# Another order of steps and of PSUM banks in the first part of an attention and Fourier-mix kernel

## Chip, cores and metric

The kernel runs on one core of a Trainium2 chip. The metric is the device time of one execution in microseconds (us), the median over several runs. Engines: TensorE (PE), VectorE (DVE), ScalarE (ACT), GpSimd (POOL) and SyncE (SP), which issues the DMAs.

## What is computed

Eight batches, eight heads, 576 positions, 64 dimensions per head; 128 random features; all float32 (the two MLP weights come as float64). First a linear attention with positive features, then a Fourier mix with residual, a layer norm and an MLP with residual:

```python
def phi(x):
    proj = np.einsum('bhsd,md->bhsm', x, omega)
    sq = np.sum(x * x, axis=-1, keepdims=True) / 2.0
    h = proj - sq
    h = h - np.max(h, axis=-1, keepdims=True)
    return np.exp(h) / np.sqrt(m)
q_p, k_p = (phi(q_s), phi(k_s))
kv = np.einsum('bhsm,bhsd->bhmd', k_p, v)
z = np.sum(k_p, axis=2)
num = np.einsum('bhsm,bhmd->bhsd', q_p, kv)
den = np.einsum('bhsm,bhm->bhs', q_p, z)[..., None] + 1e-06
x = (num / den) transposed and reshaped to (B, S, H*D)

u = x + np.real(np.fft.fft(np.fft.fft(x, axis=1), axis=2))
un = (u - mean(u)) / np.sqrt(var(u) + 1e-06)
out = u + np.maximum(un @ w_ch1, 0.0) @ w_ch2
```

## The kernel before

The kernel has two parts. Part one (to about 418 us of the profile) does the attention and the Fourier mix of all eight batches, converts the MLP's weights to float32, and does the MLP of the first four tiles of 128 rows. Part two does the MLP of the other 4096 rows in blocks, with sums of sub-blocks that save products (Strassen's way).

Part one works on 32 pairs of heads, n = 0 to 31, four to a batch. Its work is written as streams of steps: Python generators that yield a `Step` (engine, estimated duration, what it waits for, which buffers it takes and gives back) and then issue the step's instructions. The steps that matter here, with the names that the text uses and the lines at which the profile lists them:

- `T kqTn a:b`: PE transposes columns a to b of k and q of pair n into one PSUM bank (L636). ACT or DVE copies the bank to SBUF (L652, L650).
- `Sn a:b`: scores against the features (L731), four matmuls on quarters of the array for each column, or two on halves of its rows (the form R). `Sn 0:4` and `Sn 5:9` fill two banks, `Sn 4:5` is narrow but takes two banks as well. DVE takes the maximum over the features (nmx, L673: wide over two banks, or narrow), ACT the exponentials (L690), four to a bank. The banks come free behind them.
- `KVn`: 36 small matmuls (72 records) of the keys' features with v and a column of ones (L766) into two banks. ACT or DVE copies the result (L782, L780).
- `T qeTn a:b`: transposes the queries' features (L636), copied by L652 or L650.
- `NDn`: numerator and denominator (L814, L822) into two banks. DVE adds the epsilon, takes the reciprocal (rden, L831, L832) and multiplies (L843, or ACT at L839); that frees the two banks.
- `MIXb`: the Fourier mix of batch b as matmuls with tables (L933, L947, then L993, L1004), after sums on DVE and POOL (L870 to L910); DVE adds the results (L1047 to L1060).
- `Pj hf` and `Pj of`: hidden and output steps of the plain MLP of tile j (L1293, L1318), closed by an addition on DVE (L1332).
- `narrow`: the conversion of one 128x512 piece of a weight from float64, 32 pieces, on POOL or ACT (L558, L560), then DVE (L563, L565, L568, L570), then POOL or DVE (L576).
- `warm`: 12 records of matmuls on zeros at the beginning (L605).
- `norm_of`: layer norms; four transpositions on PE (L1227) for each tile of the plain MLP, and for the four tiles of block 0, the first block of part two.

The order isn't found while the kernel is built; it is written out. `Listing.run` merges the streams: at each turn `PICKS` names the stream that is next (and, where a step can run on two engines, which one), `BANKS` names the first PSUM bank that a step takes, and `FORMS`, read at each PE step by `form()`, says how the step's matmuls are cut. Each engine executes its instructions in the order in which the steps were merged, and a step whose bank or operand isn't ready holds back all that stands behind it on its engine:

```python
        while todo:
            other, n = next(picks, (None, None))
            may = []
            for item in todo if n is None else [todo[n]]:
                got = self.start(*item[2:], other, item[0] + item[2].bias if n is None else None)
                if got is not None:
                    may.append((got, item))
```

Part two has lists of its own (`PICKS2`, `BANKS2`), which the change doesn't touch.

Of the kernel before, what the change touches and what calls it, by code (L numbers as in the profile page):

```python
# [41 lines left out]
class Clock(NamedTuple):  # L42
# [23 lines left out]


PICKS = (
    "1g30geg03ghid3dddehciMfegcdgej8ijgRNd8dih3gifjhbhf8hKhebgcgcijhebkl9fdcbmbN0kidhakjjdOb7f79i9baeSdja"
    "jbbScifhjgbTgfibgdijdjhjfijfabibbjdcjdiaShjhdSfdjcbfbfjjgbb9ffcgkkekhjkQecgSiki8chifjhefadfcggQgQc9d"  # L70
    "babadgcdakOb8fha8e9gfhfgg8ff1ffdPfbecffffce9e7c7fehhhbhhhhjhb8giejTijLjj7ig978ijijecdTjih8ejgfgbQgfk"
    "f88efhkkVfllWh9k9Tb8McmallmN8jkkklllkc7lmjnhfhhmoopVjcen8eaihjSbcjdekggmjbbnlohRI9linmb89eMeggWmdlhi"
    "mkeklOkfgjgURdgjbhdldkldelgmWgehkchjgifidhbbihec9fkicjbalihhbj60ijj6L96ijji7adi7edR8kjl7k6mdceeclnPe"
    "9jpfkh3Xjin95a7mekaal8bihhklmn4jgmfj7jnH8ooeeiebeko8cg9jkbifponpkpLnkkppRccSgegmmklcldX6bebdnhhWchie"
    "dSgkcmnmG7hclLaallfkjfdjnimSiiaV9ecd8kfkcT8ejjbbh6ghfd48aggghgahgcfiPghggb6gcddgg5bdhfdeiija5LjTidcc"
    "759g9gSahNce7hefigUlggck9cljafjgelagXicL8khailaRkilgiajbgeQhb7djjgihicjkahc8dbclMkhggjjcbkjjabjkkicc"
    "d7ljlaecd7ki9c5akkVbdllkaa67Klcjl9ighi6jfj77kkjIdmm9nlmlcm9loebhbno8QinZngkf#gqnpjmjkrlmj6jqknlg9llj"
    "jicjciiolii7hcQ6cafh7hgcgk59eiibibbii7Selllcl8jjml9c58ncf7dlelfFfdnm97k7l8di5lhlmm7j7lhlmen6jiLP8lgn"
    "nnnXggmmmfnoj9okfhlop8hnpllgjgIkknn9Xhhngonen9YlhjYWlhoY7hppqhr4ahlmkhffqqkqoroeqaenkdngp9ZZ955el99j"
    "ggih5kagf9n7gnd5cqcpdhfm9m9mlaXoaiJmkm8gmgnigfnnngga5akellaVacmmkVVm74cmg5mml9hgii7lllhppm9rmpptokpo"  # L80
    "qjjmqlqIo7qdlplZmoq76qqbXooknhclijlOkhgghjgf5gemijgfPiVhjUdllkhglikigLlgkGejdiPddbjkmheenganil50WWWW"
    "ma4lhfKbj5I77fJ9Mc90bebeeef4aHeadfc5aecb5fL89hObffadfgdchhcadgfhiibKS9kbgkLhgcQa9dIcbdb77gie79I8aiJU"
    "kK3hdJ9g9469Pd6baf8efe6idiajcHTT8kdbkdiien6mNpZpPpblOeOo5hePcSkLb32aHfhiSSeeaab76eiLai3ffgbfj7difmj8"
    "68dhcfil3dgl6n7nnXmWddQickli69fdiNOgaNgc9cEdI7abehijd9kkfah5Sia5aa7e9de595cad8ac24dbccb5dNbbaae6cffc"
    "hi7LO6bJbdaaddeaPb6dacgb8bfdN9b8KdfecccFgLfPRbQSi6Rc7ijhjk31O%%%%%%tjttb12f5s1J7q8aqqq89ppF5peqj4Yde"
    "enmgoXXnXgm4njQ1lj0NmLbeo33bf0dm81Un1ehAlggl60jkkQ6jjjjkjlikl9jlmiTc9ngnla08mfncgm8ogmjmccfjabib59fe"
    "hleb7j3j49djj7g7hL7h6g6QaidiIc360ff075efg5794h7a5ged7dgEhh8ffff43a094896b9b72b2baE322267360636645544"
    "43300100"
)

BANKS = (
    "3012406207460426047614204702610424206742764064210461702606425016437042604670426420340276450214620462"
    "0154240623024602432023602476105246103240736247021640524026704672047501647240264320620340260462460262"
    "4052361420652430517205647602642064605427135703462040267450231462402456406521346062023460201026026064"
    "3172260467420642301602450647201320460345627402467064246042673402646207143672167204231602465421240643"
    "7426462740516207246121046042654723450173602660512046721451706257067312"
)

FORMS = (
# [6 lines left out]
)  # L108


# [2365 lines left out]
```

## Time and profile before

| | us |
|---|---|
| median of three runs | 1112.38 (1112.29 to 1117.94) |
| the profiled execution | 1113.75 |
| its span, from the first to the last instruction | 1112.0 |
| PE busy | 1091.5 (98%) |
| DVE busy | 882.4 (79%) |
| ACT busy | 538.7 (48%) |
| POOL busy | 389.9 (35%) |

A row of a timeline gives the start in us from the span's beginning, the time until the last of its instructions ended, engine, line, operation, output and input, shapes, the number of instructions, and in brackets the idle time of the engine ahead of it with what ended that. One matmul of the program stands as two records, a transposition as one. "issue" is time in which an engine waited for nothing that the profile shows. A row of waits gives the waiting engine and line, whom it waited for, the sum in us, how often, and the longest. Busy shares are averages over stretches with different limits, so part one is read apart from part two, and in stretches.

### The profile page before, as it was taken

The page shows a single profiled execution, that of the slowest core. Times are in us where ns is not written, and L with a number is a line of the kernel's source. Part 1 is how long each engine was busy: PE and PEld are TensorE (multiplying, and loading weights), DVE is VectorE, ACT ScalarE, POOL GpSimd, SP SyncE. Part 2 cuts the span into 40 slices and gives each one's busy share as a digit, 9 for nine tenths or more (in the row PEclk, how much of TensorE's full clock was granted, in tenths as well). Part 3 has the DMA queues.
Part 4 walks back from the last instruction along what each step waited for, and adds up shares of the span by engine and source line. Part 5 has one row for each costly group of instructions (what it writes and reads, how often), then busy time and mean ns, then how long its engine had stood idle before and what let it go on. Part 6 is the DMA issues. An engine that isn't in the chain of part 4 may idle for free.

```text
span 1112.0 us, 42246 instructions
## 1 busy us (share of the span) xinstructions
PE 1091.5 (98%) x17759; PEld 923.9 (83%) x17759; DVE 882.4 (79%) x1685; ACT 538.7 (48%) x1644; POOL 389.9 (35%) x404
## 2 busy tenths in 40 slices
PE   8899999999999999999999999999999999999998
PEld 7788888878878676799998668998667999667998
DVE  6899999996776766688697777898667898668895
ACT  6988888865725554624214453223563223341221
POOL 2343444524655537733613455000365000152000
PEclk9999999999999999999999999999999999999999
DMA  7856756566665568798798768757678756556553
GB/s 230 222 177 194 242 177 202 173 191 179 222 224 211 186 183 314 228 294 299 246 300 297 215 201 254 215 158 238 203 213 259 226 156 216 174 157 220 152 160 112
DMA packets 196590, 236.80 MB, mean 213 GB/s; under 512 B 53808, under 2 KB 120624, under 8 KB 196400
## 3 DMA queue, kind: packets, MB, share of 16 engines
q1 hardware_dynamic: 195904, 233.83, 68.3%
q8 instruction: 140, 2.29, 0.9%
q14 instruction: 50, 0.41, 0.1%
q10 hardware_dynamic: 496, 0.26, 0.1%
HBM read 182.13 MB, written 56.10 MB: 214 GB/s over the span
## 4 chain that ended last, share of the span: by engine, by line
PE 92%; ACT 3%; DVE 3%; issue 1%; DMA 1%; POOL 0%; SPq 0%; DVEq 0%; ACTq 0%; POOLq 0%
PE banks L2259 30%; PE banks L1806 27%; PE banks L731 5%; PE banks L1293 5%; PE banks L1318 5%; PE banks L636 5%; PE banks L1958 4%; PE banks L766 3%; PE banks L814 2%; ACT e L690 2%; PE banks L933 2%; PE banks L993 2%; PE banks L947 1%; DVE nmx L673 1%; PE banks L822 1%
## 5 line engine op out<-in xcount | busy, mean ns | idle before, releaser
L2259 PE MATMUL banks<-wl,sums 128*64 128x128 f32 x3584 | 217.2, 273 | 0.1
L2259 PEld LDWEIGHTS banks<-wl,sums 128*64 128x64 f32 x3584 | 201.0, 137 | 2.4 <-issue 0.5
L690 ACT ACTIVATE e<-banks,nmx 128x128 f32<-128x128 f32 x576 | 161.3, 425 | 24.3 <-DVE nmx L673 23.9
L673 DVE TENSOR_REDUCE nmx<-banks 128x8 f32<-128x1024 f32 (+1 forms) x96 | 89.3, 953 | 25.6 <-PE banks L731 21.3
L2259 PE MATMUL banks<-wl,hid 128*64 128x128 f32 x1536 | 98.4, 273 | 0.5 <-DVE part L2234 0.5
L2259 PEld LDWEIGHTS banks<-wl,hid 128*64 128x64 f32 x1536 | 87.6, 137 | 1.7 <-DVE part L2234 0.7
L1806 PE MATMUL banks<-unw,wxw 128*64 128x256 f32 x704 | 85.8, 379 | 0.0
L2229 ACT ACTIVATE s<-banks 128x128 f32<-128x128 f32 x112 | 30.9, 277 | 109.7 <-PE banks L2259 109.7
L731 PE MATMUL banks<-om,kqT 64*64 64x128 f32 (+1 forms) x1988 | 81.7, 278 | 1.2 <-ACT e L690 0.8
L731 PEld LDWEIGHTS banks<-om,kqT 64*64 64x64 f32 (+1 forms) x1988 | 67.4, 143 | 12.8 <-issue 4.7
L2259 PE MATMUL banks<-wl,hx 128*64 128x128 f32 x1152 | 73.4, 273 | 0.4 <-DVE part L2234 0.4
L1806 PE MATMUL banks<-rx,wxw 128*64 128x256 f32 x576 | 71.2, 379 | 0.0
L1806 PEld LDWEIGHTS banks<-unw,wxw 128*64 128x64 f32 x704 | 50.6, 137 | 24.7
L1806 PE MATMUL banks<-ttw,wxw 128*64 128x256 f32 x576 | 70.2, 379 | 0.0
L1831 ACT ACTIVATE s<-banks 128x512 f32<-128x512 f32 x65 | 38.5, 596 | 64.2 <-PE banks L1806 59.2
L576 POOL TENSOR_TENSOR w<-w,raw 128x512 f32<-128x512 f32 x28 | 38.3, 1372 | 86.3 <-DVE raw L570 86.3
L2259 PEld LDWEIGHTS banks<-wl,hx 128*64 128x64 f32 x1152 | 65.3, 137 | 1.2 <-DVE part L2234 0.6
L1293 PE MATMUL banks<-unT,w 128*64 128x128 f32 (+1 forms) x744 | 64.5, 276 | 0.0
L2308 POOL TENSOR_TENSOR more<-more,part 128x512 f32<-128x512 f32 x2 | 2.7, 1340 | 172.6 <-ACT part L2301 172.6
L1293 PEld LDWEIGHTS banks<-unT,w 128*64 128x64 f32 (+1 forms) x744 | 58.9, 158 | 2.5 <-issue 1.2
L1318 PE MATMUL banks<-w,ht 128*128 128x512 f32 (+1 forms) x152 | 59.0, 597 | 0.0
L1806 PEld LDWEIGHTS banks<-rx,wxw 128*64 128x64 f32 x576 | 41.4, 137 | 20.2
(289 smaller groups left out, 2387.6 us busy)
## 6 DMA issues: line engine op xcount, KB each, us to landing
wl<-w2l SPq DMA_DIRECT2D x245, 256.0 KB, 3.9
wxw<-w1x SPq DMA_DIRECT2D x120, 256.0 KB, 3.2
raw<-in_moe_w_ch_dram SPq DMA_DIRECT2D x32, 512.0 KB, 4.7
kq<-in_k_dram SPq DMA_DIRECT2D x32, 288.0 KB, 4.2
kq<-in_q_dram SPq DMA_DIRECT2D x32, 288.0 KB, 4.6
vd<-in_v_dram SPq DMA_DIRECT2D x32, 288.0 KB, 5.0
ur<-us SPq DMA_DIRECT2D x30, 256.0 KB, 4.9
w2l<-sums SPq DMA_DIRECT2D x14, 512.0 KB, 3.9
```

Of the source, the lines that this page charges most:

```text
L576: eng.tensor_tensor(out=dst, in0=dst, in1=lof, op=ALU.add)
L636: nc.tensor.transpose(ps[:, (j - j0) * 128 : (j - j0 + 1) * 128], src(j), ident[:])
L673: nc.vector.tensor_reduce(nmx[:, :, 0:num], pps[:, :, 0 : MF * num].rearrange("p b (c m) -> p b c m", m=MF), axis=AX.X, op=ALU.max, negate ...
L690: nc.scalar.activation(out=e[:, c + (i if num == 1 else 0), :], in_=pps[:, i, MF * c : MF * c + MF], func=AF.Exp, bias=nmx[:, i, c : c + 1],)
L731: nc.tensor.matmul(pps[cols, c, MF * m : MF * m + MF], lhsT=kqT[rows, j, cols], rhs=om2[rows, :],)
L766: nc.tensor.matmul(kvp[cols, i, 0 : D + 1], lhsT=feature(r)[rows, cols], rhs=vds[n % NV][rows, r, :], start=(r == 0), stop=(r == R - 1),)
L1293: nc.tensor.matmul(hp[cols, 0:TP], lhsT=w1[:, dc, 128 * fc : 128 * fc + 128][:, cols], rhs=unTs[key][:, dc, :], start=(dc == 0), stop=(dc ...
L1318: nc.tensor.matmul(yp[cols, 0:DM], lhsT=hs[fc][:, 128 * i : 128 * i + 128][:, cols], rhs=w2[:, fc, :], start=(fc == 0), stop=(fc == NFC - ...
L1806: nc.tensor.matmul(ps[half, span * f : span * f + span].rearrange("f (b q) -> f b q", q=Q), lhsT=left[:, P * f : P * f + P][:, half], rhs= ...
L1831: nc.scalar.activation(out=s[:], in_=ps, func=AF.Copy)
L1958: nc.tensor.matmul(cell[half].rearrange("f t (b q) -> f t b q", q=Q), lhsT=w[:, d, col : col + 128][:, half], rhs=right[:, :, d].rearrange ...
L2259: nc.tensor.matmul(ps[half, 0:128], lhsT=left[:, f][:, half], rhs=wls[head(j), i, n][:, f], start=start and f == 0, stop=(f == 3), skip_gr ...
```

## The change

`PICKS`, `BANKS` and `FORMS` are replaced by other strings. Each step keeps its engine and its form, and the steps on SP keep their order; `FORMS` differs only because the forms are read in the order of the PE steps. The order of steps on PE, DVE, ACT and POOL in part one changes, and so do the PSUM banks that steps take.

```diff
 PICKS = (
-    "1g30geg03ghid3dddehciMfegcdgej8ijgRNd8dih3gifjhbhf8hKhebgcgcijhebkl9fdcbmbN0kidhakjjdOb7f79i9baeSdja"
-    "jbbScifhjgbTgfibgdijdjhjfijfabibbjdcjdiaShjhdSfdjcbfbfjjgbb9ffcgkkekhjkQecgSiki8chifjhefadfcggQgQc9d"
...
+    "1g0ff2ee4f0g3ddgfcfhdNidf3dkNc7iSibdRbekbijhfj7hgijgaijjfb0fefddheb9iichidPegbcacc8bh8ic9jf8jkjSihdj"
+    "SS9eh9iiiLhefkecjfjcceagfjefhecgghfhfaRhgakbldgbhNjfbejij9abiffSgihjihhfbkegkc8achbjNcffc9fceiihfaSi"
...
 BANKS = (
-    "3012406207460426047614204702610424206742764064210461702606425016437042604670426420340276450214620462"
...
+    "4301246704624201246750461023063204062360452646020423674260643612765064206230624620360264750217420642"
...
 FORMS = (
-    "4W 2Q W R 3W 4Q 6W Q W C R 2W 2Q 3W 3Q C 3W R 2W C W 3Q 2W Q 4W 4Q C Q 7W 3Q C W WQ 3W WQ W R 2Ccz Q W 2R C 5W Q "
...
+    "4W 2Q 2W R W Q W 2Q 2W Q 4W C R Q 4W 2Q 2W 2Q C 3W Q R 2W C W 2Q W 2Q 5W 4Q C Q 7W 3Q C W WQ 3W WQ W R 2Ccz Q W "
...
```

The beginning of PE's order, read from these strings, before: T kqT0 (three steps), S0 0:4, S0 4:5, T kqT1 0:4, S0 5:9, T kqT1 4:8, warm, T kqT1 8:9, S1 0:4, S1 4:5, KV0, S1 5:9, T qeT0 (three steps). After: T kqT0 (three steps), S0 0:4, S0 4:5, T kqT1 0:4, T kqT1 4:8, S0 5:9, T kqT1 8:9, S1 0:4, warm, S1 4:5, KV0, T qeT0 0:1, T qeT0 1:5, S1 5:9, T qeT0 5:9.

More of the change, by code (lines that the diff above doesn't have):

```diff
@@ L68 @@
 PICKS = (
-    "1g30geg03ghid3dddehciMfegcdgej8ijgRNd8dih3gifjhbhf8hKhebgcgcijhebkl9fdcbmbN0kidhakjjdOb7f79i9baeSdja"
-    "jbbScifhjgbTgfibgdijdjhjfijfabibbjdcjdiaShjhdSfdjcbfbfjjgbb9ffcgkkekhjkQecgSiki8chifjhefadfcggQgQc9d"
-    "babadgcdakOb8fha8e9gfhfgg8ff1ffdPfbecffffce9e7c7fehhhbhhhhjhb8giejTijLjj7ig978ijijecdTjih8ejgfgbQgfk"
-    "f88efhkkVfllWh9k9Tb8McmallmN8jkkklllkc7lmjnhfhhmoopVjcen8eaihjSbcjdekggmjbbnlohRI9linmb89eMeggWmdlhi"
-    "mkeklOkfgjgURdgjbhdldkldelgmWgehkchjgifidhbbihec9fkicjbalihhbj60ijj6L96ijji7adi7edR8kjl7k6mdceeclnPe"
@@ L74 @@
[L74 to L88, printed above, removed]
+    "1g0ff2ee4f0g3ddgfcfhdNidf3dkNc7iSibdRbekbijhfj7hgijgaijjfb0fefddheb9iichidPegbcacc8bh8ic9jf8jkjSihdj"
@@ new lines @@
+    "SS9eh9iiiLhefkecjfjcceagfjefhecgghfhfaRhgakbldgbhNjfbejij9abiffSgihjihhfbkegkc8achbjNcffc9fceiihfaSi"
+    "cjR8gh9gi9Ta8ddiedg9hh1gdeadcbbbgechhfahLghcj6jk6efhfL7gbf7kiak6aebje7Ohh7j8bjdehiig9PgabcjcTa89gfdj"
+    "ic8gehkkgkVhhmXQm8SdmekRmakikk8ikkdjlldmlkkaenop96pqaiSefgaTi8imabnhcmcckgjTk9amQdknIiU9imnfnlnVigml"
+    "klkhWlkmnVjmmifkijiokijikmjkiaogikpdcchPgaelemQkebmleljcdj0idbaggb8cg8jj9icfd9lbbkngof7f7kjekn9WgoiL"
+    "c5agadnconn3Xg6mm947j98ehijgakkiid66kmmnedgl5mfmngnga!ifFcfhfdpfoldhoilXkhlmcdmdhKegnefep6eebohid9ff"
@@ new lines @@
+    "VSfQekgkig9Fj9kklihiiefifSljfhkcImUbg79ciUb7bbd6bgigifeidiigghii7jijTgejeehihif6jdhjadjh58b6b8lcb9k6"
+    "keibj7fLj8SjUSjaijjkkUcdffhkhmhjmjLlfhelRi9UhkilkdjbecdjThfggjl7igcihicjkfdcfajm8mNffd7k99bimklifl9b"
+    "fggdckl5cckdcm6eOj97m6mgb7fedlkfh7f8m6ngKdWcmmnmmbboc77hnpknmoij6!ggaefjhHphgogolooSfnnoncngknjnnhci"
+    "kjl76g9lgkfhkhRjehhH9a8kk5ajjjad6e5mfnel8ddli8deh8fVe5amg6ifknghXfnnfdlgkl6elinn5bnobjmngNbnjmmdmjlk"
+    "mmW758iijfkpsgijhss8iopgimqjiihmnpaKnlnkfnhokbbXghoWTkdheOhjeiilVjeon7e6kehoojfcmYnpp8kbc74pgbpeacMn"
@@ new lines @@
+    "kha7agm58bnife5comoekoc8cli6olb8jjch4lTdclack9ekQcckjgejk5glee4iVmjh8khkgclhjOomb7MjmEnoemop9afjnohf"
+    "j6okbXffdll3jjut8vvviav(ufpsqtr5ruspq7Zpor4pnmqo8JXmmtrkl!smFnpZskn9jsj0ksjllltokpl7mhlsissnjVppskTS"
+    "%%WiSiZUqkhmkjj53hmmklnoipp3hfooPlqikqk!hipXThmpjinokmjpiloqrYmpmn3dQlfmmipjhpgTlkmkomUYhijooXkknVkl"
+    "ghminhimPZpZVgXipgoplphrkVgkgkgqnookepQ$gssTqel0soesU!rodrm1UVTtafsMrncpeqqRcqjpfhbbmrspjtS&&ukmcMpq"
+    "mtlcjudvdhutfth%nkZeuq$sWueqeloTsgUgdgfreTsjonjrdgffkdfemhopiimhpekegaiefjhkhcNeleddlejmoeppSldglnoT"
@@ L89 @@
+    "VkjRhghWldnffhmmnihXjeefiWjlfkofpjfojjZNlhkijqilapramR$$s$$$$$$$$ssqssaq1n1ddsWmtiklQnqksMhdsdnjkeik"
+    "nbgPXXgmXLjmkaOim0mh069nn90I8dallVh756mmif0j04hdhjklfmN5kkkkklllk39akNhi98k7abhjj7ljilccelabgbd90fe3"
+    "e958hchbe377idb8gQeRhhbgfOg208Jb7eg07b733468c8g667fe8g7cf363dd2cc94cccdcG97456aa54278570616646466445"
+    "43300110"
 )
 BANKS = (
-    "3012406207460426047614204702610424206742764064210461702606425016437042604670426420340276450214620462"
-    "0154240623024602432023602476105246103240736247021640524026704672047501647240264320620340260462460262"
@@ L94 @@
-    "4052361420652430517205647602642064605427135703462040267450231462402456406521346062023460201026026064"
-    "3172260467420642301602450647201320460345627402467064246042673402646207143672167204231602465421240643"
-    "7426462740516207246121046042654723450173602660512046721451706257067312"
+    "4301246704624201246750461023063204062360452646020423674260643612765064206230624620360264750217420642"
+    "1672064263402340162106460217463260325620476146042406720426502450652304512642064067023462742640624012"
@@ L97 @@
+    "6016472064216701645706325264042604024713657305264020427360531462042016460524352026067520601526026052"
+    "6132620565726042017604623140632740264501236462104674260460120746202453645301725620240167043412640167"
+    "4264204156423167402650456024324675034164206246720546402314706340476310"
 )
 FORMS = (
[6 rows of a table removed]
[6 rows of a table added]
 )
```

10 rows, old and new, of the table FORMS are left out of this document.

## The prediction

> **What bounds the kernel now.** I read the page first (engines, chain), then the windows cut at the places where the load changes, then the waits of TensorE (PE) and of DVE in part one, then the timelines of PE and DVE at the longest waits. The page:
>
> ```profile
> span 1112.0 us, 42246 instructions
> ...
> PE 1091.5 (98%) x17759; PEld 923.9 (83%) x17759; DVE 882.4 (79%) x1685; ACT 538.7 (48%) x1644; POOL 389.9 (35%) x404
> ...
> q8 instruction: 140, 2.29, 0.9%
> ...
> PE 92%; ACT 3%; DVE 3%; issue 1%; DMA 1%; POOL 0%; SPq 0%; DVEq 0%; ACTq 0%; POOLq 0%
> ```
>
> PE carries 92% of the chain that ended last, so what counts is time in which PE waits. The windows (columns: length, then busy us of PE, weight loads, DVE, ACT, POOL, then granted clock) show where that is:
>
> ```profile
> 0.00:17.15 17.15, 12.49 (x232) 10.79 (x232) 6.74 (x12) 9.72 (x30) 4.11 (x15) 1.00 0.83 245
> 17.15:50.00 32.85, 30.06 (x775) 25.66 (x776) 29.50 (x52) 29.99 (x113) 12.72 (x9) 1.00 0.84 231
> 50.00:150.00 100.00, 95.87 (x2130) 83.99 (x2128) 93.91 (x211) 87.99 (x317) 42.13 (x41) 1.00 0.66 199
> 150.00:250.00 100.00, 99.97 (x2018) 84.47 (x2012) 95.25 (x217) 80.20 (x290) 43.33 (x44) 1.00 0.62 185
> 250.00:300.00 50.00, 47.54 (x1120) 43.00 (x1119) 34.90 (x68) 33.37 (x126) 30.18 (x30) 1.00 0.61 184
> 300.00:418.00 118.00, 116.80 (x1599) 87.14 (x1598) 82.06 (x208) 58.21 (x182) 53.39 (x72) 1.00 0.64 206
> ```
>
> The cut at 418 is the end of part one. Up to there PE is idle for 4.66 + 2.79 + 4.13 + 0.03 + 2.46 + 1.20 = 15.3 us, and that is all that another order could take from PE's visible waits. From 17 to 250 DVE is nearly full (29.5 of 32.9, then 93.9 and 95.3 of 100), so there PE and DVE bound together: a PE wait is worth something only where DVE waits too, and the reverse. From 150 PE is full and no order gives or takes much. What PE waits for between 17 and 418, and what DVE waits for between 17 and 150:
>
> ```profile
> PE banks L636 <- ACT e L690: 2.1, 5, 0.6
> PE banks L766 <- issue: 2.1, 3, 1.2
> PE banks L814 <- issue: 1.7, 2, 1.3
> PE banks L636 <- issue: 1.4, 1, 1.4
> PE banks L993 <- issue: 1.0, 1, 1.0
> PE banks L731 <- ACT e L690: 0.8, 2, 0.6
> PE banks L822 <- issue: 0.5, 1, 0.5
> ```
> ```profile
> DVE rden L831 <- PE banks L822: 4.4, 5, 1.6
> DVE nmx L673 <- PE banks L731: 1.3, 4, 0.5
> ```
>
> Of PE's waits 6.7 us (2.1 + 1.7 + 1.4 + 1.0 + 0.5) are "issue": PE had its operands and no instruction. The rest is mostly a transposition or a score step that wants a PSUM bank whose exponentials (L690) are not done. DVE's waits for PE sum to 5.7 us in 133 us (4.4 + 1.3), most of them for the end of an ND step (L822), which PE reached late.
>
> **The change, part by part.** Every engine executes the same instructions as before. 281 of the 498 PE steps of part one stand at another place, KV28 by 14 places, the others by at most 11; all 213 DMA issues on SP keep their places; behind part one all queues are equal. Changes between array shapes (full, column halves, quarters) number 207 in both orders, so they cost nothing new. Only waits can change.
>
> *Start (to 17 us).* PE and DVE before:
>
> ```profile
> 11.36 1.50 PE L605 MATMUL banks<-ur 128*128 128x128 f32 x12
> 12.70 0.27 PE L636 MATMUL banks<-ident,kq 128*128 128x128 f32 x1
> 12.90 1.32 PE L731 MATMUL banks<-om,kqT 64*64 64x128 f32 x40
> ```
> ```profile
> 14.36 1.56 DVE L673 TENSOR_REDUCE nmx<-banks 128x2 f32<-128x256 f32 x2 [2.15 <-ACT e L690]
> 15.83 0.28 DVE L780 COPY kv<-banks 128x130 f32<-128x130 f32 x1
> 16.03 0.42 DVE L563 TENSOR_SCALAR sign<-raw 128x512 uint32<-128x512 uint32 x1
> 17.63 1.22 DVE L673 TENSOR_REDUCE nmx<-banks 128x8 f32<-128x1024 f32 x1
> ```
>
> S1 0:4 (12.90) stood behind the warming matmuls (11.36, 1.34 us from their start to 12.70), and DVE idled 2.15 us until the scores of head pair 1 came (the row names ACT, but S1's matmuls end at 12.90 + 1.32 = 14.22, just ahead of 14.36). Now S1 0:4 stands ahead of them. Its start falls from 12.90 to about 11.55, so DVE gets its first wide maximum near 12.75 instead of 14.70 (the second of the two at 14.36). Not all of the 2.15 us is won: the eviction of T kqT1 0:4 now stands ahead of the first wide maximum and waits some 0.6 us for PE, and the KV0 copy waits some 0.45. The maximum at 17.63 stays where it was, but 1.1 us more of weight conversion is then behind DVE. So -1.1, between -2.15 (all of the wait) and 0. S1 5:9 moves behind two transpositions; its maximum (17.63) is covered by that conversion, and by up to 1.1 us no longer if the conversion's data are late.
>
> *17 to 50 us.* DVE's waits here:
>
> ```profile
> 36.51 0.17 DVE L831 TENSOR_SCALAR rden<-banks 128x10 f32<-128x10 f32 x1 [0.63 <-PE banks L822]
> 42.09 1.23 DVE L673 TENSOR_REDUCE nmx<-banks 128x8 f32<-128x1024 f32 x1 [0.26 <-PE banks L731]
> 47.50 1.23 DVE L673 TENSOR_REDUCE nmx<-banks 128x8 f32<-128x1024 f32 x1 [0.26 <-PE banks L731]
> 50.35 0.17 DVE L831 TENSOR_SCALAR rden<-banks 128x10 f32<-128x10 f32 x1 [1.62 <-PE banks L822]
> ```
>
> T qeT2 1:5 and 5:9 now stand ahead of S3 4:5, so ND2 (36.51) has its operands earlier; S4 4:5 and a transposition stand ahead of KV3, which had waited for ND2's two banks; S4 5:9 (42.09) moves up ahead of T qeT3. I count the waits of 0.63, 0.26 and 0.26 as gone: -1.15. The 1.62 stays: ND3 stands at the same place behind the same number of instructions, and its own matmuls stopped on an instruction:
>
> ```profile
> 49.26 0.74 PE L814 MATMUL banks<-kv,qeT 128*64 128x65 f32 x18 [1.29 <-issue]
> ```
>
> Against that I set +0.4: near 24 us DVE's queue now holds both evictions of kqT3 ahead of a maximum, with PE reaching those transpositions later. Bounds: -2.8 (all four waits) to +1.2 (another 0.63 twice, and none gone).
>
> *50 to 150 us.* 5.7 - 2.77 leaves some 2.9 us of DVE's waits for PE. Order and work ahead of each maximum hardly change up to 82. S8 5:9 moves up one transposition:
>
> ```profile
> 84.73 1.23 DVE L673 TENSOR_REDUCE nmx<-banks 128x8 f32<-128x1024 f32 x1 [0.54 <-PE banks L731]
> ```
>
> So -0.5. Between 82 and 133 us most steps are exchanged with neighbours (13 of 48 score steps before 150 stand later, 11 earlier); I take 0 for that, between -2.4 (the rest of the 2.9) and +3 (as much again).
>
> *150 to 418 us.* PE's 99.97 of 100 until 250 leaves 0. From 250 PE idles 3.7 us, and three "issue" waits (1.4, 1.0, 1.2 in the table) are 3.6 of it. They come where many small matmuls follow each other. 17759 matmuls and as many weight loads over 140 fetches are 254 instructions each, 127 matmuls. KV29 and KV31 (72 matmuls each) still stand together, S28, KV26 and S28 too. KV25 and KV23 are parted somewhat; KV28, ND26 and ND27 (72 + 40 + 40) are brought together. 0, between -1.5 and +2.
>
> [...]
>
> *The seam.* The last of block 0's transpositions (L1227) moves behind one more output step. DVE's sums on it were done early:
>
> ```profile
> 413.69 0.29 DVE L1418 TENSOR_TENSOR tt<-unT,tt 128x128 f32<-128x128 f32 x1
> 418.15 0.69 DVE L1332 TENSOR_TENSOR ur<-ur,banks 128x512 f32<-128x512 f32 x1 [4.17 <-PE banks L1318]
> ```
> ```profile
> 405.93 12.18 PE L1318 MATMUL banks<-w,ht 128*128 128x512 f32 x28
> ```
>
> One output step is 12.18 / 7 = 1.7 us, inside the 4.17 us of cover: 0. Without the cover up to +1. MIX7's first products move behind three hidden steps of P3; PE's later output steps cover its sums. Part two begins with PE's last output step in either order and is not changed: 0.
>
> **The sum.** -1.1 - 1.15 + 0.4 - 0.5 = -2.35, say -2.4. The profiled execution took 1113.75 us (span 1112.0 and 1.75 around it), which would become 1111.4. It stands 1.4 us above the median of the runs, 1112.38, and from that I forecast 1110.0. What a measurement can tell from no change is about 0.5%, 5.6 us: under 1106.8 or over 1117.9.
>
> **Rivals.** *Fetch waits go.* If the interleaving lets the fetches keep ahead, ND3's 1.29 and the 3.6 us after 250 go too: -2.4 - 4.9 = -7.3, 1105.1. For it: they are 6.7 us of PE's waits. Against it: at ND3, KV29/KV31 and S28/KV26 the runs of small matmuls are nearly the same. [...] Chance 0.15 (a gain over 5.6 us).
>
> *The waits only change places.* DVE is 94% full, a bank freed sooner for one step is taken from another, and KV28 + ND26 + ND27, 152 matmuls, bring one fetch wait more, 1.3 us like the longest of L814. Then the lead isn't got: 1112.38 + 1.3 = 1113.7. For it: the number of steps moved up and down is about equal. Chance 0.25.
>
> *Slower: DVE starves on score steps set back.* Each score step that stands behind a step still waiting for a bank holds back the maximum, and with it exponentials, KV and ND. In the stretch of 17 to 150, 13 of 48 are set back; at 0.5 us each (the 0.54 and the 0.63 above) that is 6.5 us, 1112.38 + 6.5 = 1118.9. It decides for slower when DVE's waits from 17 to 150 for PE exceed some 12 us, against 5.7. For it: S3 4:5 goes back four places, S10 4:5 three. Against it: only single places for most, and 11 are moved up. Chance 0.10.
>
> **How the numbers follow.** My forecast (a gain of 0.5 to 5) has 0.50. Faster than 0.5%: 0.15, the first rival. Slower: 0.10. Within: 0.50 + 0.25 = 0.75. The ends of the terms' ranges won't all meet: from -6.5 to +3.6 leaves out about 1 in 10 on each side, 1105.9 to 1116.0.
>
> **What would show it.** Right: the warming matmuls (L605) behind S1 and DVE's wait of 2.15 near 14 us under 1.2; DVE's waits for PE from 17 to 150 near 4; PE still 99.9 of 100 afterwards; PE's last output step of part one ending at 415.6 instead of 418; "issue" still near 6.7. Wrong: part one ending after 418, or ending earlier with part two longer than the 694 us from 418 to 1112; "issue" halved (first rival) or DVE's waits doubled (third).

## The result, and the profile after

The changed kernel is slower: 1118.07 us median (1114.56 to 1121.44, 15 runs) against 1113.01 (1111.91 to 1117.94, 15 runs) for the kernel before, a ratio of 1.0041 with a 95% interval of 1.0028 to 1.0054. The forecast was 1110.0 with a range of 1105.9 to 1116.0; the measured time lies above it. The profiled execution took 1115.64 us (span 1113.8), one of the shortest of the 15, so its trace shows the lesser part of the loss.

The windows of the changed kernel, cut as before (length, busy us of PE, weight loads, DVE, ACT, POOL, then granted clock, DMA share, GB/s):

```profile
0.00:17.15 17.15, 12.95 (x236) 11.05 (x236) 7.95 (x14) 9.64 (x31) 4.12 (x15) 1.00 0.94 275
17.15:50.00 32.85, 30.57 (x851) 26.27 (x843) 30.54 (x53) 31.06 (x118) 12.74 (x9) 1.00 0.80 216
50.00:150.00 100.00, 96.81 (x2153) 84.58 (x2143) 95.01 (x213) 87.60 (x315) 43.37 (x43) 1.00 0.64 199
150.00:250.00 100.00, 99.23 (x1956) 83.28 (x1956) 94.66 (x215) 79.50 (x283) 45.47 (x47) 1.00 0.61 186
250.00:300.00 50.00, 49.28 (x1114) 44.80 (x1111) 31.96 (x66) 34.77 (x136) 25.17 (x26) 1.00 0.64 194
300.00:418.00 118.00, 114.76 (x1569) 84.16 (x1568) 90.27 (x208) 54.94 (x173) 56.81 (x71) 1.00 0.63 201
```

Up to 300 us PE idles less than before in sum (11.2 against 14.1 us), though from 150 to 250 it idles more (0.77 against 0.03). From 300 to 418 its busy time falls from 116.80 to 114.76, and DVE's rises from 82.06 to 90.27 with the same number of instructions, 208, nearly all of the same kinds: several of them last longer there. The five largest waits of PE in part one behind its first matmul (engine, line, whom it waits for: us in total, times, longest):

```profile
PE banks L636 <- ACT e L690: 2.2, 5, 0.6
PE banks L731 <- DVE kqT L650: 1.8, 3, 1.3
PE banks L766 <- issue: 1.6, 2, 1.1
PE banks L731 <- issue: 1.1, 1, 1.1
PE banks L814 <- issue: 1.0, 1, 1.0
```

"L731 <- DVE kqT L650" is new. The next table follows PE by steps instead of by lines. It gives the start of PE's n-th step (its first matmul in the timeline) in the first profile of before, and how many us earlier the other kernels begin their n-th step (a negative number: later); e1 to e13 are the experiments below. At each of these steps the same steps lie behind PE in both orders, but for step 397: there the changed order has done KV28 and a transposition in place of an output step of P1 and another transposition, a difference of some 0.3 us. L2379 is the first instruction of part two.

| PE's step | before | before again (e12) | changed | changed again (e1) | e2 | e3 | e6 | e9 | e13 |
|---|---|---|---|---|---|---|---|---|---|
| 60 | 50.17 | 0.42 | 1.26 | 0.93 | -0.44 | -0.99 | -0.36 | 0.59 | 0.36 |
| 153 | 123.21 | 0.48 | 3.32 | 2.67 | 1.44 | -0.43 | 1.24 | 2.74 | 1.71 |
| 363 | 284.52 | 0.83 | 3.32 | 1.22 | 1.37 | 0.52 | -0.21 | 3.23 | -2.62 |
| 397 | 315.41 | 1.06 | 2.53 | 0.97 | 1.84 | -0.81 | -0.18 | 2.09 | -2.09 |
| 421 | 339.34 | 1.05 | -1.02 | -2.75 | 1.84 | -4.63 | -6.75 | 0.56 | -3.14 |
| L2379 | 417.95 | 0.93 | -0.55 | -2.06 | 0.86 | -3.95 | -6.13 | 0.67 | -3.05 |

The changed kernel led by 3.3 us at step 363 (281 us) and lost 3.6 us between its steps 397 and 421. Two places make most of that loss (1.31 and 1.09 us of waiting). The first, in PE's timeline (start, us, engine, line, shapes, count, and in brackets the idle time ahead):

```profile
322.68 0.60 PE L636 MATMUL banks<-ident,e 128*128 128x128 f32 x4
323.21 0.43 PE L731 MATMUL banks<-om,kqT 64*64 64x128 f32 x2
324.95 1.21 PE L731 MATMUL banks<-om,kqT 64*64 64x128 f32 x35 [1.31 <-DVE kqT L650]
```

S30 0:4 issues two records into its first bank and stops. By `BANKS` its second bank, 3, is still held by T kqT29 8:9, which waits for its copy (L650) on DVE. DVE's and POOL's timelines:

```profile
318.43 1.21 DVE L870 TENSOR_TENSOR half<-x 128x1024 f32<-128x1024 f32 x1
319.56 0.34 DVE L650 COPY qeT<-banks 128x64 f32<-128x64 f32 x2
319.83 2.87 DVE L872 COPY half<-x 128x2 f32<-128x2 f32 x1
322.62 0.68 DVE L876 TENSOR_TENSOR half<-half 128x510 f32<-128x510 f32 x1
323.21 1.48 DVE L876 TENSOR_TENSOR half<-x 128x255 f32<-128x255 f32 x1
324.62 0.28 DVE L650 COPY kqT<-banks 128x128 f32<-128x128 f32 x1
```
```profile
320.19 1.26 POOL L1544 TENSOR_TENSOR big<-w,big 128x512 f32<-128x512 f32 x1
321.41 1.26 POOL L1544 TENSOR_TENSOR sums<-big 128x512 f32<-128x512 f32 x1
322.75 1.66 POOL L1544 TENSOR_TENSOR sums<-big,sums 128x512 f32<-128x512 f32 x1
324.38 1.45 POOL L1544 TENSOR_TENSOR sums<-big 128x512 f32<-128x512 f32 x1
```

A copy of two columns takes 2.87 us. It ends where POOL pauses, between 322.67 (321.41 + 1.26) and 322.75, and the copy of kqT29 stands behind it and two more sums. In the kernel before, DVE's L870 took 3.54 us (1.21 in the row above) while POOL ran two sums of weights from 321.72 to 324.21, but S30 0:4 was done by then (DVE had just taken its maximum):

```profile
320.61 1.23 DVE L673 TENSOR_REDUCE nmx<-banks 128x8 f32<-128x1024 f32 x1 [4.19 <-PE banks L731]
321.76 3.54 DVE L870 TENSOR_TENSOR half<-x 128x1024 f32<-128x1024 f32 x1
```

The change set S30 0:4 back eight places (from PE's step 400 to 408). It also set the copy behind both steps of these sums, where before it stood behind the first alone, and POOL now runs four sums of weights there instead of two. The second place is an instruction wait inside S29 0:4:

```profile
335.49 1.23 PE L766 MATMUL banks<-vd,e 64*64 64x65 f32 x72
336.54 0.60 PE L731 MATMUL banks<-om,kqT 64*64 64x128 f32 x11
338.23 0.88 PE L731 MATMUL banks<-om,kqT 64*64 64x128 f32 x21 [1.09 <-issue]
```

### The profile page after: what moved, and what is told of

Same layout as the page of the kernel before. It is cut to its first block, busy times and chain, and to the rows that moved or that the text cites. A ratio compares the mean times of both kernels' runs of the same rounds, so it can differ in the third digit from the quotient of the medians.

```text
span 1113.8 us, 42230 instructions
## 1 busy us (share of the span) xinstructions
PE 1093.0 (98%) x17759; PEld 957.6 (86%) x17759; DVE 889.7 (80%) x1685; ACT 536.5 (48%) x1644; POOL 391.1 (35%) x404
## 4 chain that ended last, share of the span: by engine, by line
PE 92%; DVE 4%; ACT 2%; issue 1%; DMA 1%; DVEq 0%; ACTq 0%
PE banks L2259 30%; PE banks L1806 27%; PE banks L731 5%; PE banks L636 5%; PE banks L1293 5%; PE banks L1318 5%; PE banks L1958 4%; PE banks L766 3%; PE banks L814 3%; PE banks L993 2%; PE banks L933 2%; ACT e L690 1%; PE banks L947 1%; DVE nmx L673 1%; PE banks L822 1%
## 5 line engine op out<-in xcount | busy, mean ns | idle before, releaser
L2259 PE MATMUL banks<-wl,sums 128*64 128x128 f32 x3584 | 219.6, 273 | 0.1
L2259 PEld LDWEIGHTS banks<-wl,sums 128*64 128x64 f32 x3584 | 203.9, 137 | 1.6 <-issue 0.5
L690 ACT ACTIVATE e<-banks,nmx 128x128 f32<-128x128 f32 x576 | 161.2, 435 | 19.0 <-DVE nmx L673 18.1
L731 PE MATMUL banks<-om,kqT 64*64 64x128 f32 (+1 forms) x1988 | 82.2, 279 | 3.5 <-DVE kqT L650 1.8
L731 PEld LDWEIGHTS banks<-om,kqT 64*64 64x64 f32 (+1 forms) x1988 | 66.9, 143 | 14.3 <-issue 4.5
L1806 PEld LDWEIGHTS banks<-unw,wxw 128*64 128x64 f32 x704 | 60.8, 137 | 14.6
L1293 PEld LDWEIGHTS banks<-unT,w 128*64 128x64 f32 (+1 forms) x744 | 58.7, 158 | 3.8 <-issue 2.6
L1806 PEld LDWEIGHTS banks<-rx,wxw 128*64 128x64 f32 x576 | 49.7, 137 | 12.0
L1806 PEld LDWEIGHTS banks<-ttw,wxw 128*64 128x64 f32 x576 | 49.7, 137 | 12.0
```

The costliest lines, as they stand in the source:

```text
L690: nc.scalar.activation(out=e[:, c + (i if num == 1 else 0), :], in_=pps[:, i, MF * c : MF * c + MF], func=AF.Exp, bias=nmx[:, i, c : c + 1],)
L731: nc.tensor.matmul(pps[cols, c, MF * m : MF * m + MF], lhsT=kqT[rows, j, cols], rhs=om2[rows, :],)
L1293: nc.tensor.matmul(hp[cols, 0:TP], lhsT=w1[:, dc, 128 * fc : 128 * fc + 128][:, cols], rhs=unTs[key][:, dc, :], start=(dc == 0), stop=(dc ...
L1806: nc.tensor.matmul(ps[half, span * f : span * f + span].rearrange("f (b q) -> f b q", q=Q), lhsT=left[:, P * f : P * f + P][:, half], rhs= ...
L2259: nc.tensor.matmul(ps[half, 0:128], lhsT=left[:, f][:, half], rhs=wls[head(j), i, n][:, f], start=start and f == 0, stop=(f == 3), skip_gr ...
```

## The experiments

In the diffs a line is a step or a stretch of PE's order. Where a stretch is taken from the other kernel, all engines' steps that belong to it are, and the banks are renamed consistently.

**e1 to e4: which stretch costs the time?** e1 is the changed kernel again.

> The changed kernel once more, unaltered. Theory (the loss lies in part one, between 281 and 374 us, where the changed order gives back 3.6 us of lead): part one ends 0.4 to 0.8 us later than before's 418, part two is as long as before's to within the spread, and the time stays some 4 to 5 us over the kernel before, of which part one explains under 1 us. Rival (part two is longer behind the changed part one, though its instructions and their order are the same): part one ends near 418.5 again, and part two is 3 us or more longer than the 694 us of before. Rival (clock): the granted clock is 0.997 to 0.998 in most runs of this kernel and 1.000 in those of the kernel before; 0.0025 of 1092 us is 2.7 us.

1117.59 us, ratio 1.0043 (1.0028 to 1.0058). The loss between steps 397 and 421 is there again (3.7 us); part one ended 2.1 us later than before's, where the theory said 0.4 to 0.8. Part two took 1114.8 - 420.0 = 694.8 us: no more than the 694.0 of before within the spread of the profiles here (693.6 to 695.5, and 697.5 in e10, where the granted clock was 0.53 from 570.05 to 573.05), so the rival with a longer part two falls. The rival with the clock has something: in the changed kernel's 22 runs so far, 15 had a mean granted clock under 0.9985, against 4 of 29 runs of before. One place that it comes from is seen in PE's timeline and the windows of e1:

```profile
47.97 0.80 PE L814 MATMUL banks<-kv,qeT 128*64 128x65 f32 x13 [1.96 <-issue]
```
```profile
44.00:48.00 4.00, 1.85 (x50) 1.54 (x50) 2.60 (x5) 4.00 (x18) 1.28 (x1) 1.00 0.94 270
48.00:52.00 4.00, 4.00 (x98) 3.76 (x99) 2.48 (x6) 0.94 (x4) 0.00 (x0) 0.57 0.06 19
52.00:56.00 4.00, 3.79 (x81) 3.34 (x83) 3.86 (x9) 3.79 (x14) 0.97 (x1) 1.00 0.79 219
```

PE waited 1.96 us for instructions in ND3, and then ran 4 us at a granted clock of 0.57; in stretches of 0.5 us it was 0.50 from 48.5 to 51.5. At 0.5 the loss is that of 3.4 us of half clock (0.43 x 4 / 0.5), by estimate 1.7 us of PE's time.

```diff
 PE's steps   1 to 362: changed order
-PE's steps 363 to 498: changed order
+PE's steps 363 to 498: order of before
```

> The changed order for PE's first 362 steps (to S26 5:9, 281 us in the changed kernel), the order of before for the other 136, with the banks renamed consistently; part two as it is. Theory (lead of 3.3 us got by 281 us, lost between there and 374 us by the order of that stretch): the lead is kept, part one ends at 414.7 instead of 418, and the time is 3.3 us under before, 1109.7. Rival (the lead meets a bound that any order has in that stretch, loads or DVE): part one ends at 417.5 to 418, time 1113. Rival (part two reacts to the moved part one, not to this stretch): part two over 697 us and a time over 1113.

1112.36 us, ratio 0.9990 (0.9974 to 1.0007). The lead isn't lost behind step 363 any more (1.37 there, 1.80 at the last output step, 0.86 at L2379), so the first theory holds in kind. Its numbers missed: the lead itself was 1.4 us in this execution, not 3.3, part one ended at 417.09 instead of 414.7, and no gain can be told from these runs.

```diff
-PE's steps   1 to 362: changed order
+PE's steps   1 to 362: order of before
 PE's steps 363 to 498: changed order
```

> The other half alone: the order of before for PE's first 362 steps, the changed order for the last 136. Theory: no lead is got and 3.9 us are lost between 284 and 378 us, so part one ends at 421.8 and the time is 1117. Rival (a bound that any order has there): part one ends at 418 to 418.5, time 1113. Rival (part two is longer behind the changed end of part one): part one ends near 418.5 to 422 and part two takes over 697 us.

1116.12 us, ratio 1.0029 (1.0019 to 1.0039): the changed end alone costs 2.9 us. Part one ends at 421.90, as the theory gave it. PE's waits from 284 to 421.9 us, the five largest:

```profile
PE banks L731 <- issue: 1.4, 1, 1.4
PE banks L731 <- DVE kqT L650: 1.3, 1, 1.3
PE banks L1293 <- issue: 0.9, 1, 0.9
PE banks L1318 <- issue: 0.8, 1, 0.8
PE banks L766 <- issue: 0.3, 1, 0.3
```

The first two are S29 0:4 and S30 0:4. The fourth stands behind KV28, ND26 and ND27.

```diff
-PE's steps 231 to 362: order of before
+PE's steps 231 to 362: changed order
```

> Only PE's steps 231 to 362 (180 to 281 us) in the changed order, before and behind them the order of before. In that stretch the changed kernel gained 1.5 us: PE's wait of 1.55 us for an instruction at a transposition near 268 us wasn't there. Theory (fetch stalls hang on which instructions stand together): that wait is gone here too, part one ends 1.5 us earlier, at 416.5, and the time is 1111.5. Rival (the fetches are placed by chance or by the start of the stretch): the issue waits stay within 0.3 us of before's 6.7 and the time is 1113.

1112.86 us, ratio 1.0000 (0.9987 to 1.0014). No gain of its own. From 180 to 284 us PE still waits 1.5 us for instructions, in two places (0.8 and 0.7) instead of one (1.4). Part one ends at 418.10, after 0.78 us of waiting for P3's last addition.

**e5 and e6: single steps of the changed end.**

```diff
 DVE, changed kernel:
+copy of T kqT29 8:9                                (L650)
 sums for MIX6, second half, steps 1 and 2          (L870 to L876)
-copy of T kqT29 8:9                                (L650)
 closing addition of P1                             (L1332)
```

> The changed kernel with one step moved on DVE alone: the copy of T kqT29 8:9 stands ahead of the second pair of DVE's sums for MIX6 (L870 to L876) instead of behind them. In the changed kernel S30 0:4 stops for 1.3 us at 324 us, because one of its two banks is still held by that transposition, whose copy waits on DVE behind a sum that takes 2.9 us where it normally takes 0.16. Theory (bank held by a copy behind a slow sum): PE's wait of 1.3 us at L731 for DVE's L650 is gone, part one ends 1.3 us earlier than in the two profiles of the changed kernel (417.2 to 418.7 instead of 418.5 to 420.0), the time falls from 1117.8 to 1116.5. Rival (the wait only moves to the maximum of S30, which DVE then reaches as late as before): part one ends within 0.3 us of the changed kernel's.

1117.16 us, ratio 1.0045 (1.0028 to 1.0061): no gain; the rival is right in kind. PE's wait at S30 0:4 is gone, and PE meets the next bank that stands behind the sums, that of P1's output, and the granted clock behind it is 0.65:

```profile
328.17 0.76 PE L947 MATMUL banks<-cs_sb,fold 64*64 64x320 f32 x6 [2.44 <-DVE ur L1332]
```
```profile
328.00:332.00 4.00, 3.83 (x34) 3.23 (x36) 3.90 (x9) 1.45 (x5) 0.00 (x0) 0.65 0.02 4
```

```diff
 PE, changed kernel:
+ND28
 MIX6, second product
-ND28
 S30 5:9, KV30, S29 0:4
```

> The changed kernel with two neighbours on PE exchanged: ND28 ahead of MIX6's second product instead of behind it, so that ND28, S30 5:9, KV30 and S29 0:4 don't stand together. Theory (many small matmuls in a row outrun the instruction fetch): PE's issue wait of 1.1 to 1.4 us inside S29 0:4 falls under 0.5, part one ends about 1 us earlier, the time falls from 1117.8 to 1116.8. Rival (the stall sits at a place in the instruction stream, whatever stands there): an issue wait of over 1 us within 2 us of the same place. Rival (ND28 moved up waits for its two banks): PE waits for ACT's L690 at L814.

1118.31 us, ratio 1.0040 (1.0023 to 1.0058). The instruction wait in S29 0:4 is gone. That doesn't prove the theory: with PE's order of the changed kernel this wait was 1.1 to 1.2 us in its two profiles, but 0.28 in e5. And ND28 now waits 0.9 us for its banks (L690), as the second rival had it. This execution shows how bad S30 0:4 can get; up to there all queues are those of the changed kernel:

```profile
329.24 1.73 PE L731 MATMUL banks<-om,kqT 64*64 64x128 f32 x35 [2.90 <-DVE kqT L650]
```
```profile
321.20 4.64 DVE L870 TENSOR_TENSOR half<-x 128x1024 f32<-128x1024 f32 x1
```
```profile
330.00:334.00 4.00, 4.00 (x50) 2.94 (x44) 2.63 (x5) 0.63 (x2) 0.00 (x0) 0.60 0.02 4
```

2.90 us of wait, 4 us at a clock of 0.60 behind it, and 6.6 us lost from step 397 to step 421, where the changed kernel's own profile lost 3.6.

**e7 and e8: the start.**

```diff
-PE's steps   1 to  80: changed order
+PE's steps   1 to  80: order of before
 PE's steps  81 to 362: changed order
-PE's steps 363 to 498: changed order
+PE's steps 363 to 498: order of before
```

> Before's order for PE's first 80 steps (to 67 us), the changed order for steps 81 to 362, before's for the rest. It is the kernel with the changed first 362 steps, with the start undone. Theory (the changed start makes the halved clock likely: PE's issue wait at ND3 near 46 us lasts 1.0 to 2.0 us, and behind one of 1.96 and one of 1.73 us the granted clock was 0.5 to 0.6 for some 4 us): at most 2 runs of 12 show a mean granted clock under 0.9985, as with before's start so far (6 of 52 runs), against 5 of 12 with the changed start and before's end. Time: the gain of 67 to 281 us without that of the start, some 1 to 1.5 us, 1111.5. Rival (the lower clock comes from a denser PE later): as many runs with a lower clock as with the changed start.

1111.86 us, ratio 0.9994 (0.9979 to 1.0009), 3 of 12 runs with the lower clock: one more than the theory's 2, and fewer than the 5 of e2. In the time there is no difference to e2 or to before that these runs can tell.

```diff
 PE's steps   1 to  80: changed order
-PE's steps  81 to 498: changed order
+PE's steps  81 to 498: order of before
```

> The reverse: the changed order for PE's first 80 steps, before's for all others. Theory (the start sets the halved clock): 4 to 8 runs of 12 show a mean granted clock under 0.9985, and these are about 2 us longer than the others; the start's own gain of 1.4 us in the profile is lost in such runs, so the median is 1112.5 to 1114. Rival (clock from later work): at most 2 runs of 12 under 0.9985 and a time of 1111.5.

1112.62 us, ratio 0.9991 (0.9979 to 1.0003), 4 of 12 runs with the lower clock, as the theory's lower end; but these runs were not longer than the others (median 1112.45 against 1112.62). By themselves these two runs leave the start's effect on the clock open.

**e9 to e13: mending the stall.** In e9 whatever PE waits for goes ahead of the sums on DVE; all other queues are those of the changed kernel.

```diff
 DVE, changed kernel:
-sums for MIX6, second half, steps 1 and 2          (L870 to L876)
 copy of T kqT29 8:9, closing addition of P1, two maxima of S30
+sums for MIX6, second half, steps 1 and 2          (L870 to L876)
 sums for MIX6, second half, steps 3 and 4
```

> The changed kernel with DVE's first two steps of sums for MIX6's second half (L870 to L876) moved behind the copy of T kqT29 8:9, P1's closing addition and the two maxima of S30. In the changed kernel and in the two kernels before this one, one of these sums took 2.9 to 4.4 us while POOL ran its sums without a pause, and what stood behind it on DVE held a PSUM bank that PE wanted: 1.3 us at S30 0:4, 2.4 us at MIX6's first product when only the copy was moved. Theory (nothing that PE waits for stands behind that sum any more): no PE wait for DVE between 315 and 335 us, part one ends 1.6 us earlier (416.9 to 418.4), and as no stall there can halve the clock, at most 6 of 12 runs show a mean granted clock under 0.9985 (35 of 45 in the three kernels with both changed halves); time 1115.5. Rival (DVE is late whatever stands first): a wait of 1 us or more for DVE comes at MIX6's second product, and the time stays at 1117 to 1118.

1113.50 us, ratio 1.0008 (0.9996 to 1.0020). Two steps moved on DVE take back some 4 us of the 5, more than the 2 expected. DVE's timeline: the copy at once, the sums later, the first two in 1.22 and 0.17 us, as at other places (1.22 and 0.16 in before at 51.66 and 52.80).

```profile
319.44 0.29 DVE L650 COPY kqT<-banks 128x128 f32<-128x128 f32 x1 [0.23 <-PE banks L636]
326.57 1.22 DVE L870 TENSOR_TENSOR half<-x 128x1024 f32<-128x1024 f32 x1
327.70 0.17 DVE L872 COPY half<-x 128x2 f32<-128x2 f32 x1
```

No wait for L650 or L1332 is left, and PE loses 1.5 us from step 397 to 421 instead of 3.6; the instruction wait in S29 0:4 is 0.4 here. 6 of 11 runs had the lower clock (a mean under 0.9985), against 35 of 45 in the changed kernel, e1, e5 and e6.

```diff
 as e9, and on PE:
+ND28
 MIX6, second product
-ND28
```

> As the kernel before this one, and ND28 ahead of MIX6's second product, so that ND28, S30 5:9, KV30 and S29 0:4 don't stand together. Theory: no wait of 1 us or more for DVE or for instructions between 315 and 345 us; part one ends 1 us earlier than with the sums moved alone (416 to 417.4), time 1114.5. Rival (ND28 waits for its two banks, 0.9 us for ACT's L690 when it was exchanged alone): that wait stays, and the time is that of the kernel with the sums moved alone.

1114.43 us, ratio 1.0018 (1.0005 to 1.0031). The rival: ND28 waits 0.9 us for L690, and from step 397 to 421 1.6 us are lost, as in e9. The instruction wait was only exchanged.

```diff
 as e9, and
-PE's steps   1 to  80: changed order
+PE's steps   1 to  80: order of before
```

> Before's order for PE's first 80 steps, the changed order for all others, and the sums moved as in the first kernel of this group. Theory (two places make the stalls that halve the clock: ND3 near 46 us with the changed start, S30 near 324 us with the changed end): with both gone at most 3 of 12 runs show a granted clock under 0.9985; the fetch wait at S29 0:4 and the lead of 67 to 281 us remain; time 1113.5 to 1114.5. Rival (a third place): 6 or more of 12 runs with a lower clock.

1113.70 us, ratio 1.0018 (1.0007 to 1.0030), 2 of 12 runs with the lower clock, as the theory had it. The profiled execution is one of the two: behind an instruction wait of 2.02 us at 260 us, a third place, the granted clock was 0.74 from 259.94 to 262.94.

> The kernel before, unaltered, for a second profile of it. In the profiles of two kernels that execute before's order to 180 us, PE reached its step 60 (50 us) 0.9 us earlier and 1.0 us later than in the one profile of before. Theory (the lead of 1.3 us that the changed start shows at that step is as large as what differs from one execution to the next): this profile reaches step 60 between 49.2 and 51.2 us and part one ends between 416.9 and 418.9. Rival (before's profile was typical): within 0.2 us of 50.17 and 417.95.

The second profile of before begins step 60 at 49.75 us (0.42 earlier) and part two at 417.02 (0.93 earlier). So one profile of before is as good as the next to about 1 us, and a lead of 1 us in one profile is no gain yet.

```diff
 changed kernel:
-four sums of weights (L1544) on POOL, from 320.2 us
+the same four on DVE, behind its sums for MIX6
```

> The changed kernel with four sums of weights (L1544) executed on DVE, behind its other work of that stretch, instead of on POOL; DVE's queue ahead of the copy of T kqT29 8:9 and PE's order are as in the changed kernel. In the changed kernel POOL ran them from 320.2 to 325.8 us without a pause, while DVE's sums L870 to L876 for MIX6's second half, 2.2 us of work in other places, took from 318.4 to 324.7. Theory (DVE's sum stands still as long as POOL runs one sum behind the other): these sums now take under 3 us from the first to the last, the copy follows them, PE's wait of 1.3 us or more at S30 0:4 falls under 0.3, and the time comes to 1113 to 1114.5, as with the sums moved behind on DVE. Rival (the sum waits for something else, its input or a transfer): it takes as long as before, PE waits 1 us or more for DVE's L650 at S30 0:4, and the time stays at 1117 to 1118.

1113.53 us, ratio 1.0005 (0.9996 to 1.0014). Without those four sums on POOL, DVE's sums take 3.05 us from 323.39 to 326.44, with a copy among them (the theory said under 3), the copy of kqT29 follows, and PE has no wait for it:

```profile
323.39 1.52 DVE L870 TENSOR_TENSOR half<-x 128x1024 f32<-128x1024 f32 x1
325.10 0.42 DVE L872 COPY half<-x 128x2 f32<-128x2 f32 x1
326.37 0.27 DVE L650 COPY kqT<-banks 128x128 f32<-128x128 f32 x1
```
```profile
327.82 1.32 PE L731 MATMUL banks<-om,kqT 64*64 64x128 f32 x40
```

The theory holds, and from the other side: DVE's order is untouched ahead of the copy, and the stall is gone with POOL's sums. The profiled execution of e13 is its slowest run (1117.11; a granted clock of 0.64 from 48.96 to 51.96, and of 0.50 from 131.82 to 134.82), so its span is not compared.

No version beats the kernel before by more than its interval; the nearest are e2 (0.9990), e8 (0.9991) and e7 (0.9994).

## Why the prediction was wrong

**The step that failed: the term for 150 to 418 us ("0, between -1.5 and +2").** From its step 363 (281 us) to the end of part one the changed kernel lost 3.9 us in its own profile. I had written "From 150 PE is full and no order gives or takes much"; but this full PE lost what new stalls took (1.31 and 1.09 us at the two places above). Of this stretch I weighed only PE's instruction waits and the block KV28, ND26, ND27. That block did cost a wait at L1318 (0.3 us in the changed kernel, 0.8 in e3) where the rival said 1.3. The loss came from S30 0:4, which I had not priced, through a chain over three engines: POOL's sums hold up DVE's (2.87 us for a copy of two columns, 0.42 in e13), the copy behind them holds a bank, the score step wants the bank. Undoing either end of the chain (e9 on DVE, e13 on POOL) brings the time to 1113.5, so this chain is worth about 4 of the 5 us. In the traces it is 1.3 to 1.4 us of waiting in the changed kernel, e1 and e3, and 2.9 in e6 with a granted clock of 0.59 over the 3 us behind it. That the unprofiled runs mix these two cases is an inference: their traces weren't taken. What is left (e9 and e13 against before: 1.1 and 0.9 us, both intervals include no change) is not taken apart further. Between steps 363 and 421, with the same steps done in every kernel, the six profiles with before's end take 54.2 to 54.8 us, the changed kernel, e1 and e3 58.8 to 60.0, e13 55.4, but e9, e10 and e11 still 57.1 to 57.5. In these single profiles the quiet POOL takes back nearly all of that stretch and the sums moved on DVE less than half, though the median times of e9 and e13 are equal.

The third rival named the mechanism, a score step that stands behind a step still waiting for a bank, but looked for it between 17 and 150 us, priced it at 0.5 us for each of 13 steps, and gave it 0.10. It was one step, at 323 us, at 1.3 to 2.9. That its 1118.9 lies close to the measured 1118.07 is luck: its own sign, DVE's waits for PE over 12 us from 17 to 150, came out at 3.7.

**Start, -1.1, and 17 to 50 us, -0.75 in sum.** The mechanism came as forecast. The warming matmuls (L605, 12.34) stand behind S1 0:4 (10.96), and DVE's wait near 14 us fell from 2.15 to 1.02:

```profile
14.45 0.42 DVE L673 TENSOR_REDUCE nmx<-banks 128x2 f32<-128x256 f32 x1 [1.02 <-PE banks L731]
```

DVE's waits for PE between 17 and 150 sum to 3.7 us (forecast: near 4; before 5.7, and 5.9 with a line of 0.2 that the prediction left out):

```profile
DVE rden L831 <- PE banks L822: 2.5, 4, 1.4
DVE kqT L650 <- PE banks L636: 0.5, 2, 0.3
DVE nmx L673 <- PE banks L731: 0.4, 2, 0.2
DVE ht L1275 <- PE banks L1293: 0.3, 1, 0.3
```

Up to ND3 the nine profiles with the changed first 80 steps lead the first profile of before by 1.26 us on average (-0.12 to 2.23), and the six with before's by 0.0 (-1.99 to 1.19). The mis-sized term is ND3's: "The 1.62 stays", 1.29 of it "issue". The instruction wait at ND3 was 0.7 to 2.8 us in those nine profiles (median 2.0) and 0 to 1.3 in the six (0 to 2.0 with the waits in the KV steps ahead of it), and in five of the nine the granted clock was 0.50 to 0.64 over the 3 us behind it. Some 11 us later, at step 73, the averages are 0.26 and 0.65: the early lead is gone.

**50 to 150 us, -0.5.** About as forecast, within a wide spread: from step 73 to step 206 (58.7 to 162.5 us) the ten profiles with the changed order there gain 0.8 on average (-1.8 to 1.8) on the first profile of before, the four others with before's order 0.2 (-0.1 to 0.6). The two that lose, e6 and e13, waited 1.9 and 2.0 us for instructions near 132 us.

**Seam, 0.** Right: L2379 follows the last output step without a wait in the changed kernel. But part one ends at 418.50 instead of 415.6, behind 418, as the prediction named for its being wrong.

**Granted clock.** I took 1.00 from the windows of one profile and gave it no term. Counted over all runs, the mean was under 0.9985 in 65 of 103 runs with the changed first 80 steps (35 of 45 with the stall at S30 besides, 30 of 58 without it) and in 18 of 154 with before's (the kernel before itself 11 of 107). In the changed kernel these runs have a median of 1118.89, the others 1116.68. In e8 and e2 they are not longer, so the 2.2 us can't all be laid to the clock; and e13, with 9 of 11 such runs, still came to 1113.5.

**The first rival.** "Issue" neither halved nor vanished: 4.5 us of PE's waits from 17 to 418, against 6.7 before. Part two kept its length, as the prediction assumed.

## What to carry to other kernels

Before a step is set back, read for each PSUM bank that it takes who gives the bank back and what stands ahead of that on the giver's queue, also where that engine is far from full: DVE was busy 82 of 118 us here. Put copies that free banks ahead of long sums between SBUF tiles, above all where POOL runs its own sums at the same time: the copy of two columns took 2.87 us here, 0.16 in before with POOL idle. And a stall of PE has two prices here: 1.3 us cost 1.3 (granted clock 1.00 behind it), while 1.6 us and more mostly (11 times of 13) cost the stall and, by estimate, another 1.7 us (half of the 3.41 us at a clock of 0.50).

## What the runs showed of the hardware

**Behind most waits of PE of 1.6 us and more the granted clock was 0.50.** In the fifteen profiles PE stood idle for over 0.9 us 45 times behind its first matmul. Of the 13 waits of 1.61 us and more, 11 were followed by a granted clock of 0.50 to 0.74 over the next 3 us; behind the two others, of 1.93 and 1.86 us (one in e6 near 132 us, one in e9 near 49 us), it was 1.00. Of the 32 waits of 0.9 to 1.56 us none was followed by a clock under 1.00. Behind each of the 11 waits the granted clock was 0.50 for 3.41 us (in e1: 0.77 from 48.0 to 48.5, 0.50 to 51.5, 0.82 to 52.0). Why it stayed at 1.00 behind the waits of 1.93 and 1.86, no run here shows.

**DVE and POOL hold each other up.** In the changed kernel a DVE copy of 128x2 took 2.87 us. It went on over two of POOL's instructions in a row, 320.19 to 322.67, and ended at 322.70, in a pause of 0.08 us between two of POOL's sums. It took 0.16 us in before, where POOL ran nothing from 324.21 to 332.02, and 0.42 in e13, where it ended with POOL's last instruction (323.79 + 1.70 = 325.49):

```profile
323.79 1.70 POOL L1060 TENSOR_TENSOR x<-x,bmp 64x255 f32<-64x255 f32 x1
```

POOL was slower beside DVE as well: in the changed kernel its sums of 128x512 took 1.26 us at 320.19 and at 321.41, and 1.66 at 322.75, while DVE's L876 ran from 322.62 to 324.69. What makes them slower together, no run here shows.

**The "issue" waits of PE end behind a packet of the instruction queue.** In the fifteen traces PE has 51 "issue" waits of over 0.6 us in part one. Each ends 1.20 to 1.62 us after a packet of the instruction queue q8 has ended; in before, for one, a packet of 16384 bytes ran from 46.76 to 47.64, and ND3 went on at 49.26. Up to 420 us the packets of q8 end 6.2 us apart there in the median. That PE waited for the instructions in these packets is an inference. Why some packets come late and others in time, no run here shows.
